# Attention, experts and an MLP on one core: a small add moves from VectorE to ScalarE, and eight low parts and four word steps get other places

## Chip, cores, metric

The kernel runs on one core of one Trainium2 chip. The metric is the device time of one execution in microseconds (us). Engines are named as the profile names them: PE is TensorE's matmul, PEld its weight load, DVE is VectorE, ACT is ScalarE, POOL is GpSimd, SP is SyncE, whose queue issues most DMAs.

## What is computed

Three layers follow one another: attention with 32 global rows and a window of 32, a router with 8 experts of limited capacity, and an MLP. Cut to what matters:

```python
def sm(s):
    e = np.exp(s - np.max(s, axis=-1, keepdims=True))
    return e / (np.sum(e, axis=-1, keepdims=True) + 1e-09)
...
x = attention(q, k, v).transpose(0, 2, 1, 3).reshape(1152, 512)   # 2 batches, 544 + 32 rows
expert = argmax(x @ w_gate, axis=1)                               # 8 experts
# each expert takes its first 288 tokens, in order
h = np.maximum(np.einsum('ecd,edf->ecf', disp, w1), 0.0)          # 512 -> 1024
y = np.einsum('ecf,efd->ecd', h, w2)                              # 1024 -> 512
x = gate * y[expert, position]
h = x @ w_in                                                      # 512 -> 2048
g = np.where(h >= 1, h, np.where(h <= -1, 0.0, (h + 1) ** 2 / 4))
out = g @ w_out                                                   # 2048 -> 512
```

The `1e-09` in the softmax is the number that the change is about; it is added to the sums of the local rows.

## The kernel before

The order of the work is written out by hand; no scheduler moves it, and each engine runs its instructions in the order of the program.

**Attention** (0 to 84 us in the trace) is a loop over 16 steps k (two batches, pairs of row tiles, pairs of heads), with scores of step k+2, exponentials of step k+1, and values of step k-1 beside each other. Two tables, `first[k]` and `plan[k]`, hang further work on a step. One kind of it is routing: `route(k, b, tp)` puts on step k the logits and `recips` (L505 to 508: the softmax sums `SUM` of one row tile, 128 x 16, get 1e-9 added at L507 and are inverted at L508, both on DVE), then `choose` (which expert), and on steps k+1 and k+2 `x_rows` (rows of x, scaled by the inverted sums), `slots` (each token's place), and `scatter` (L566: an indirect DMA on POOL's queue that writes a tile's tokens to `xd` in DRAM, sorted by expert). There are routes at k = 7, 10 and 13, and a last one behind the loop. `x_turn` (L487) transposes attention rows into `px` in PSUM, and `evac_t` (L356) copies transposed tiles out of PSUM.

**Expert weights.** Matmuls run on pairs of a rounded high part and a remainder: a raw weight piece (512 KB, DMA by `weight_load`, L205 on SP) is rounded to `H` (`weight_h`, L218) and `L = raw - H` is taken by `weight_l` (L230, tile 128 x 1024). The pieces of the first expert, `wq[0]` to `wq[7]`, are loaded at steps 2 to 9 and converted at steps 5 to 12, one piece to a step, high part on ACT and low part on POOL. The raw pieces go through four buffers in turn, so a load waits for the low part that used its buffer. Behind the loop `weight_load(2, c)` issues the four pieces of the second expert's first matrix.

**Experts** (92 to 254 us) run one after another. The first expert's tokens `xt0` are read back from `xd` (L714) as soon as the scatters up to (1, 2) have landed; the tokens of the last two tiles go in by a matmul with `place` (L739). `X0` is the pair of high and low part of these tokens, the low part at L744 on DVE. The scatters of the last two tiles, (1, 3) and (1, 4), stand behind it. The second expert's tokens `xt1` (L778, on SP, behind two weight pieces `raw3_0` and `raw3_1`) are turned at L798 (`mx`), which stands in PE's order in the middle of the first expert's second matmul.

**MLP** (254 us to the end) takes its weights from 64-bit floats: `wide_abs` (L248, ACT), four word steps (`wide_words`: L259, L262, L265, L270, DVE, from `raw` over `ca` to `co`; `ca` and `co` have two buffers each), `wide_h` (L280, ACT) and `wide_l` (L285, DVE). The last word steps of pieces 4 and 5 of group 0 hang on the last expert, as the list `ws[2]`, whose last two entries are L270 of these two pieces. Right behind them come the tokens' high parts (L1137, ACT, in two halves) and low parts (L1138, DVE, two instructions, one tile `oldH`), and then the first matmuls `up` (L1156), `half_relu` (L1161), `g_rows`, `g_parts` and `down` (L1196). The low parts of L1138 come into `up` as its last terms.

```python
        if 5 <= k < 13:                      # loop over steps
            c = k - 5
            weight_h(*wq[c], nc.scalar)
            weight_l(*wq[c], nc.gpsimd)
    for c in range(4):                       # behind the loop
        weight_load(2, c)
    recips(1, 3, NB_)
```

Of the kernel before, what the change touches and what calls it, by code (L numbers as in the profile page):

```python
# [8 lines left out]
F32 = mybir.dt.float32  # L9
# [4 lines left out]
AF = mybir.ActivationFunctionType  # L14
# [4 lines left out]
P = 128  # L19
# [9 lines left out]
def tile_attention_moe_ffn(  # L29
# [23 lines left out]
    nc = tc.nc  # L53
# [18 lines left out]
    const = ctx.enter_context(tc.tile_pool(name="const", bufs=1))  # L72
# [14 lines left out]
    def ps_tile(tag, name, hold=False):  # L87

        bank = psum[tag].pop(0)
        (held.setdefault(name, []) if hold else psum[tag]).append(bank)  # L90
        return pspool.tile([P, 512], F32, tag=bank, name=name, bufs=2 if bank == "T" else 1)
# [11 lines left out]
    def ps_v(name, hold=False):  # L103
        return ps_tile("V", name, hold)
# [56 lines left out]
    tri_b = const.tile([P, P], BF16, name="tri_b")  # L161
    ones_b = const.tile([P, P], BF16, name="ones_b")
    half = const.tile([P, 1], F32, name="half")
    racc = const.tile([P, E], BF16, name="racc")
    base_b = const.tile([P, E], BF16, name="base_b")

# [34 lines left out]
    def weight_load(u, c):  # L201
        src, n1 = units[u]
        n = n1 // 4
        raw = raw_tile(f"raw{u}_{c}")
        nc.sync.dma_start(raw.rearrange("p (k f) -> p k f", k=n), src[:, c * n:(c + 1) * n, :])  # L205
        RAW[u, c] = raw
# [15 lines left out]
    def weight_h(u, c, eng):  # L222
        if c == 0:
            unit_tiles(u, units[u][1])
        round_to(eng, HL[u][0][:, c * 1024:(c + 1) * 1024], RAW[u, c])

    def weight_l(u, c, eng):
        H, L = HL[u]
        sl = slice(c * 1024, (c + 1) * 1024)
        eng.tensor_tensor(out=L[:, sl], in0=RAW.pop((u, c)), in1=H[:, sl].bitcast(F32), op=ALU.subtract)  # L230
# [273 lines left out]

    def recips(b, lo, hi):  # L505
        sv = SUM[b][:, lo - 1:hi - 1, :]
        nc.vector.tensor_scalar_add(sv, sv, 1e-9)  # L507
        nc.vector.reciprocal(sv, sv)  # L508

    def choose(b, lo, hi):  # L510
# [90 lines left out]
    def consts():  # L601
        nc.gpsimd.tensor_copy(tri_b, tri_f)
        nc.gpsimd.memset(ones_b, 1.0)
        nc.gpsimd.memset(half, 0.5)
        nc.gpsimd.memset(racc, 0.0)
        nc.gpsimd.tensor_scalar(out=base_b, in0=iota_sb[:, :E], scalar1=float(XS), scalar2=None, op0=ALU.mult)
        for b in range(B):
            nc.gpsimd.memset(LG[b], 0.0)
            nc.gpsimd.memset(M8[b], 0.0)
            nc.gpsimd.memset(I8[b], 255)  # L610
# [33 lines left out]
    wq = [(u, c) for u in range(2) for c in range(4)]  # L644
# [14 lines left out]
    def route(k, b, tp):  # L659

        lo, hi = (0, 3) if tp == 0 else (3, 5)
        i = 2 * tp + 1
        x = [lambda j=j: x_rows(b, j) for j in range(lo, hi)]
        sc = [lambda j=j: scatter(b, j) for j in range(lo, hi)]
        first[k] += [lambda: logits(b, i, 2), lambda: recips(b, i, i + 2)]
        plan[k] += [lambda: logits_t(b, i, 2)]
        if tp == 0:
            first[k].append(lambda: logits(b, 0, 1))
            plan[k].append(lambda: logits_t(b, 0, 1))
        plan[k] += [lambda: choose(b, lo, hi)]  # L670
        first[k + 1] += x[:1]
        plan[k + 1] += [lambda: slots(b, lo, hi)] + x[1:2] + sc[:1]
        plan[k + 2] += x[2:] + sc[1:]

    route(7, 0, 0)
    route(10, 0, 1)
    route(13, 1, 0)
    plan[NS - 1] += [lambda hp=hp: last_logits(hp) for hp in range(NHP - 2)]
    for k in range(NS):
        if 0 < k < NS - 1:  # L680
            exps(k + 1)
        if 0 < k < NS - 2:
            scores(k + 2)
        for f in first[k]:
            f()
        transp(k)
        evac_t(k)
        if k > 0:
            av(k - 1)
        for f in plan.get(k, ()):  # L690
            f()
        if 2 <= k < 10:
            weight_load(*wq[k - 2])
        if 5 <= k < 13:
            c = k - 5
            weight_h(*wq[c], nc.scalar)
            weight_l(*wq[c], nc.gpsimd)
    for c in range(4):
        weight_load(2, c)
    recips(1, 3, NB_)  # L700
    for i in (3, 4):
# [43 lines left out]
    for i in (3, 4):  # L745
        scatter(1, i)

    pc = ps_v("pcnt")
    nc.tensor.matmul(pc[:1, :E], ones_b[:, 0:1], racc, start=True, stop=True)
    cnt = const.tile([1, E], I32, name="cnt")  # L750
# [239 lines left out]
    def job_l(u, c):  # L990
        weight_l(u, c, nc.vector)
        if wn[0] < len(wl) + 6:
# [8 lines left out]
    ws = [wide_words((0, 2 * c), (0, 2 * c + 1)) for c in range(3)]  # L1001
    hl = [[lambda c=c: wide_h(0, c), lambda c=c: wide_l(0, c)] for c in range(4)]
    ab = [lambda c=c: wide_abs(0, c) for c in range(8)]
    WIDE = {
        E - 2: [[], [], [], [], [], [], ab[:2], ws[0][:4]],
        E - 1: [ws[0][4:], ab[2:3], hl[0] + ab[3:4] + ws[1][:2], hl[1] + ws[1][2:4], ws[1][4:6], ws[1][6:],
                ab[4:6] + hl[2] + hl[3], ws[2]],
    }
    own = {1: [own_start], 2: [next_w], 3: [next_w], 4: [lambda: own_ones(0)], 5: [own_gated, next_w],
           6: [lambda: own_matrix(0), next_w]}  # L1010
# [122 lines left out]
    for h in range(2):  # L1133
        px = OWN["x"][h].rearrange("p (k n) -> p k n", k=2)
        xh, xl = (x.rearrange("p (a h) n -> p h a n", h=2)[:, h] for x in XC[0])
        for i in range(2):
            nc.scalar.copy(xh[:, i], px[:, i])  # L1137
        nc.vector.tensor_tensor(out=xl, in0=px, in1=xh.bitcast(F32), op=ALU.subtract)  # L1138

    nfl = fq // P  # L1140
    assert nfl == len(parts)
# [267 lines left out]
```

## Time and profile before

| | us |
|---|---|
| median of 3 runs | 464.36 |
| the three runs | 463.87 to 465.65 |
| the profiled execution's own time | 465.16 |
| its span in the trace | 463.4 |

| stretch of the trace | what runs |
|---|---|
| 0 to 84 us | attention, with routing and the first expert's weights |
| 84 to 92 us | the last tokens' routing, first expert's tokens |
| 92 to 254 us | eight experts |
| 254 to 463 us | MLP |

How to read the rows below. A row of the timeline gives start and length in us, engine, line, operation, tiles out<-in, and how many instructions were put together; in brackets is the idle time before it on its engine and what ended it. A row by stretches gives the stretch, its length, the busy us of each engine (with instructions in brackets), then the granted clock of TensorE as a share of full speed, the busy share of the DMA engines and GB/s. A row of DMA issues gives KB and median us from issue to landing. In a row of DMA landings the three numbers are least, median and most.

### The profile page before, as it was taken

To read this page: it belongs to the slowest core of one execution; us is meant where nothing else is said; L and a number is where in the kernel's file an instruction comes from. 1 tells how busy PE (TensorE), PEld (TensorE's weight loads), DVE (VectorE), ACT (ScalarE), POOL (GpSimd) and SP (SyncE) were. 2 spreads that over 40 slices of the span, in tenths; PEclk is the share of its full clock that TensorE was granted. 3 is DMA by queue.
4 is the path that set the end of the run, shared out by engine and by line. 5 is a ranking of instruction groups with operands and counts; after the bars stand their busy time and mean duration, and the time that the engine had idled before them with its cause. 6 is when DMAs were issued, how large, how long until landed. Compare 5 with 4: busy or idle time off the path is not lost. (4 is left out here: it accounts for less than half of the span.)

```text
span 463.4 us, 8110 instructions
## 1 busy us (share of the span) xinstructions
PE 445.2 (96%) x2875; PEld 375.6 (81%) x2876; DVE 335.9 (72%) x715; ACT 242.6 (52%) x508; POOL 95.5 (21%) x98
## 2 busy tenths in 40 slices
PE   8998989999999999999999899998999999999997
PEld 4876777787577777777777799998999899999996
DVE  3787698584157389946898976687888988879633
ACT  4869666173145478726766575645344344533321
POOL 1105365300000000000001543232133131322321
PEclk9999999999999999999999899999999999999999
DMA  8999554589439189963987340562321410000103
GB/s 271 298 330 340 204 181 138 172 302 374 141 123 317 34 278 343 383 248 117 341 298 243 98 149 0 201 208 93 91 75 63 136 47 1 0 2 0 69 0 127
DMA packets 34595, 79.17 MB, mean 171 GB/s; under 512 B 3761, under 2 KB 8497, under 8 KB 34546
## 3 DMA queue, kind: packets, MB, share of 16 engines
q1 hardware_dynamic: 31698, 70.40, 44.4%
q0 software_dynamic: 1408, 4.46, 3.0%
q10 hardware_dynamic: 1440, 3.67, 2.2%
q8 instruction: 29, 0.48, 0.4%
q14 instruction: 20, 0.16, 0.1%
HBM read 63.77 MB, written 14.75 MB: 169 GB/s over the span
## 5 line engine op out<-in xcount | busy, mean ns | idle before, releaser
L1156 PE MATMUL fh<-oldH,H 128*128 128x256 f32 (+1 forms) x256 | 65.9, 333 | 3.4 <-DVE oldH L1138 1.7
L230 DVE TENSOR_TENSOR L<-raw,H 128x1024 fp32r<-128x1024 f32 x56 | 66.3, 1218 | 0.9 <-ACT H L218 0.6
L1196 PE MATMUL acc<-oldH,H 128*128 128x256 f32 (+2 forms) x240 | 65.0, 332 | 1.4 <-ACT H L280 1.0
L218 ACT CAST H<-raw 128x1024 fp32r<-128x1024 f32 x57 | 58.0, 1049 | 10.3 <-PEq L895 8.4
L1156 PEld LDWEIGHTS fh<-oldH,H 128*128 128x128 f32 x256 | 46.0, 195 | 6.6 <-DVE oldH L1138 2.2
L1170 DVE SCALAR_TENSOR_TENSOR r<-r 128x256 f32<-128x256 f32 (+2 forms) x48 | 31.8, 662 | 22.1 <-ACT r L1161 21.7
L1196 PE MATMUL acc<-oldH,L 128*128 128x256 f32 (+2 forms) x144 | 47.3, 328 | 0.0
L1182 ACT CAST oldH<-g 128x256 fp32r<-128x256 f32 (+2 forms) x36 | 17.9, 496 | 55.8 <-DVE g L1174 55.8
L1196 PEld LDWEIGHTS acc<-oldH,H 128*128 128x128 f32 x240 | 43.3, 189 | 4.2 <-ACT H L280 1.5
L1156 PE MATMUL fh<-oldH,L 128*128 128x448 f32 (+1 forms) x128 | 42.3, 331 | 0.0
L1183 POOL TENSOR_TENSOR oldH<-g,oldH 128x256 fp32r<-128x256 f32 (+2 forms) x24 | 26.5, 1104 | 74.6 <-ACT oldH L1182 59.1
L599 DVE TENSOR_TENSOR hl<-pt,hh 128x512 fp32r<-128x512 f32 (+1 forms) x24 | 15.7, 654 | 35.6 <-ACT hh L598 35.6
L860 PE MATMUL py<-H,hh 128*128 128x512 f32 (+1 forms) x96 | 38.7, 403 | 0.0
L1161 ACT ACTIVATE r<-fh,half 128x256 f32<-128x256 f32 (+2 forms) x48 | 27.1, 564 | 20.6 <-PE fh L1156 17.8
L860 PE MATMUL py<-L,hh 128*128 128x512 f32 (+1 forms) x96 | 37.6, 392 | 0.0
L285 DVE TENSOR_TENSOR L<-co,H 128x512 fp32r<-128x512 f32 x32 | 23.2, 730 | 18.1 <-ACT H L280 17.4
L845 ACT ACTIVATE hs<-ph 128x512 f32<-128x512 f32 (+1 forms) x24 | 14.4, 598 | 41.2 <-PE ph L842 41.2
L1156 PE MATMUL fh<-oldL,H 128*128 128x384 f32 x128 | 35.3, 340 | 0.1
L931 POOL DMA_INDIRECT yg_own<-yd,idx x2 | 2.3, 1156 | 148.5 <-DVE hl L599 148.2
L324 ACT ACTIVATE sm<-sm,ng 128x224 f32<-128x224 f32 x64 | 30.1, 476 | 4.6 <-DVE ng L313 4.6
L270 DVE SCALAR_TENSOR_TENSOR co<-raw,ca 128x512 uint32<-128x512 uint32 x32 | 31.6, 995 | 0.9
L860 PE MATMUL py<-H,hl 128*128 128x512 f32 (+1 forms) x96 | 28.5, 401 | 0.0
(202 smaller groups left out, 1019.4 us busy)
## 6 DMA issues: line engine op xcount, KB each, us to landing
raw<-in_w_dram SPq DMA_DIRECT2D x64, 512.0 KB, 5.9
raw<-in_w_in_dram SPq DMA_DIRECT2D x14, 512.0 KB, 5.0
raw<-in_w_out_dram SPq DMA_DIRECT2D x12, 512.0 KB, 3.7
xd<-zero SPq DMA_DIRECT2D x16, 256.0 KB, 6.0
vt<-in_vx_dram SPq DMA_DIRECT2D x8, 320.0 KB, 5.0
xt<-xd SPq DMA_DIRECT2D x8, 256.0 KB, 6.3
yd<-zero SPq DMA_DIRECT2D x8, 256.0 KB, 3.8
yd<-ys SPq DMA_DIRECT2D x8, 256.0 KB, 5.2
```

What stands on the lines that cost most here:

```text
L218: nc.scalar.copy(dst, src)
L230: eng.tensor_tensor(out=L[:, sl], in0=RAW.pop((u, c)), in1=H[:, sl].bitcast(F32), op=ALU.subtract)
L270: nc.vector.scalar_tensor_tensor(out=o, in0=lo, scalar=29, in1=a, op0=ALU.logical_shift_right, op1=ALU.bitwise_or)
L285: nc.vector.tensor_tensor(out=L[:, sl], in0=CV.pop((g, c)), in1=H[:, sl].bitcast(F32), op=ALU.subtract)
L324: nc.scalar.activation(SM[s][:, c, :], SM[s][:, c, :], AF.Exp, bias=NG[s][:, c:c + 1], scale=-1.0, accum_out=SUM[b][:, i, col:col + 1])
L860: nc.tensor.matmul(py[:rows], h[:, 4 * q + k, :rows], w[:, 4 * q + k, :], start=q == i == 0, stop=q == 1 and i == len(terms) - 1)
L1156: nc.tensor.matmul(ph[:, :n], w[:, k, :], XC[c][i // 2][:, k, :], start=n_ == 0, stop=n_ == len(terms) - 1)
L1161: nc.scalar.activation(RS[f % 2][:, :n], ph[:, :n], AF.Relu, bias=half, scale=0.5)
L1170: nc.vector.scalar_tensor_tensor(out=r[:, :n], in0=r[:, :n], scalar=1.0, in1=r[:, :n], op0=ALU.min, op1=ALU.mult)
L1182: nc.scalar.copy(gh[:, :n], gt[:, :n])
L1183: nc.gpsimd.tensor_tensor(out=gl[:, :n], in0=gt[:, :n], in1=gh[:, :n].bitcast(F32), op=ALU.subtract)
L1196: nc.tensor.matmul(a[:, :n], p[:, ds], q, start=f == 0 and i == 0, stop=f == nfl - 1 and i == 2)
```

## The change

Four edits. (1) The add of 1e-9 in `recips`, four times in the program, becomes an activation on ACT (Identity, with a bias tile `tiny` that POOL fills once at the start); the reciprocal stays on DVE. (2) The high and low parts of the first expert's pieces move from steps 5 to 12 to steps 5, 6, 8, 9, 11, 12, 14 and 15, so that steps 7, 10 and 13, where routes begin, have none. The eighth low part goes to DVE, behind `X0`. (3) `weight_load(2, 3)`, whose buffer this eighth low part frees, follows it. (4) The last word step of pieces 4 and 5 moves behind the low parts L1138.

```diff
+    tiny = const.tile([P, 1], F32, name="tiny")
...
     def recips(b, lo, hi):
         sv = SUM[b][:, lo - 1:hi - 1, :]
-        nc.vector.tensor_scalar_add(sv, sv, 1e-9)
+        nc.scalar.activation(sv, sv, AF.Identity, bias=tiny)
         nc.vector.reciprocal(sv, sv)
...
+        nc.gpsimd.memset(tiny, 1e-9)
...
+    conv_at = [5, 6, 8, 9, 11, 12, 14, 15]
     route(7, 0, 0)
     route(10, 0, 1)
     route(13, 1, 0)
...
-        if 5 <= k < 13:
-            c = k - 5
+
+        if k in conv_at:
+            c = conv_at.index(k)
             weight_h(*wq[c], nc.scalar)
-            weight_l(*wq[c], nc.gpsimd)
-    for c in range(4):
+            if c < 7:
+                weight_l(*wq[c], nc.gpsimd)
+    for c in range(3):
         weight_load(2, c)
...
     for i in (3, 4):
         scatter(1, i)
 
+    weight_l(*wq[7], nc.vector)
+    weight_load(2, 3)
...
-                ab[4:6] + hl[2] + hl[3], ws[2]],
+                ab[4:6] + hl[2] + hl[3], ws[2][:6]],
...
         nc.vector.tensor_tensor(out=xl, in0=px, in1=xh.bitcast(F32), op=ALU.subtract)
+    for f in ws[2][6:]:
+        f()
```

Lines behind the edits stand one or more lines lower in the kernel after (L566 is L567 there, L230 is L231, L1138 is L1145).

**POOL, steps 9 to 16 of attention.** `raw1_0` to `raw1_3` are the pieces `wq[4]` to `wq[7]`; `xr10` is tile 0 of batch 1. Before:

```order
L566 DMA xd_77<-xr02_917,sidx_138 16384x512
L230 TENSOR_TENSOR L1_928<-raw1_0_661,H1_927 128x1024
L230 TENSOR_TENSOR L1_928<-raw1_1_746,H1_927 128x1024
L566 DMA xd_77<-xr03_1023,sidx_138 16384x512
L230 TENSOR_TENSOR L1_928<-raw1_2_863,H1_927 128x1024
L566 DMA xd_77<-xr04_1089,sidx_138 16384x512
L230 TENSOR_TENSOR L1_928<-raw1_3_925,H1_927 128x1024
L566 DMA xd_77<-xr10_1219,sidx_138 16384x512
L566 DMA xd_77<-xr11_1268,sidx_138 16384x512
L566 DMA xd_77<-xr12_1301,sidx_138 16384x512
```

After:

```order
L567 DMA xd_77<-xr02_917,sidx_139 16384x512
L231 TENSOR_TENSOR L0_583<-raw0_3_580,H0_582 128x1024
L567 DMA xd_77<-xr03_1019,sidx_139 16384x512
L231 TENSOR_TENSOR L1_1091<-raw1_0_663,H1_1090 128x1024
L567 DMA xd_77<-xr04_1085,sidx_139 16384x512
L231 TENSOR_TENSOR L1_1091<-raw1_1_748,H1_1090 128x1024
L567 DMA xd_77<-xr10_1217,sidx_139 16384x512
L231 TENSOR_TENSOR L1_1091<-raw1_2_863,H1_1090 128x1024
L567 DMA xd_77<-xr11_1266,sidx_139 16384x512
L567 DMA xd_77<-xr12_1301,sidx_139 16384x512
```

A low part now stands between the scatters of `xr10` and `xr11`, where before the three stood together, and the pair of low parts behind `xr02` is one.

**SP, behind the loop.** `xt0` and `xt1_0` are the first and second expert's tokens, `raw2_*` and `raw3_*` the second expert's weight pieces. Before:

```order
L205 DMA raw2_2_1318<-in_w1_dram 128x1024
L205 DMA raw2_3_1320<-in_w1_dram 128x1024
L714 DMA xt0_1352<-xd_77 128x512
L205 DMA raw3_0_1452<-in_w2_dram 128x2x512
L205 DMA raw3_1_1454<-in_w2_dram 128x2x512
L778 DMA xt1_0_1456<-xd_77 128x512
L205 DMA raw3_2_1458<-in_w2_dram 128x2x512
```

After:

```order
L206 DMA raw2_2_1319<-in_w1_dram 128x1024
L719 DMA xt0_1351<-xd_77 128x512
L206 DMA raw2_3_1431<-in_w1_dram 128x1024
L206 DMA raw3_0_1454<-in_w2_dram 128x2x512
L206 DMA raw3_1_1456<-in_w2_dram 128x2x512
L785 DMA xt1_0_1458<-xd_77 128x512
L206 DMA raw3_2_1460<-in_w2_dram 128x2x512
```

`raw2_3` moved behind `xt0`; it waits for the eighth low part, and `raw3_0`, `raw3_1` and `xt1_0` are queued behind it.

**DVE, end of the last expert and start of the MLP.** `ca0_4` to `ca0_6` and `co0_4`, `co0_5` are word tiles of pieces 4 to 6, `po0` and `po1` the tokens in PSUM, `oldH2` where their parts go. Before:

```order
L265 SCALAR_TENSOR_TENSOR ca0_5_3984<-raw16_5_3628,ca0_5_3984 128x512
L270 SCALAR_TENSOR_TENSOR co0_4_4006<-raw16_4_3601,ca0_4_3982 128x512
L270 SCALAR_TENSOR_TENSOR co0_5_4008<-raw16_5_3628,ca0_5_3984 128x512
...
L1138 TENSOR_TENSOR oldH2_4227<-po0_4016,oldH2_4227 128x2x256
L1138 TENSOR_TENSOR oldH2_4227<-po1_4017,oldH2_4227 128x2x256
L259 TENSOR_SCALAR ca0_6_4306<-ca0_6_4306 128x512
```

After:

```order
L1145 TENSOR_TENSOR oldH2_4225<-po0_4014,oldH2_4225 128x2x256
L1145 TENSOR_TENSOR oldH2_4225<-po1_4015,oldH2_4225 128x2x256
L271 SCALAR_TENSOR_TENSOR co0_4_4243<-raw16_4_3603,ca0_4_3984 128x512
L271 SCALAR_TENSOR_TENSOR co0_5_4245<-raw16_5_3630,ca0_5_3986 128x512
L260 TENSOR_SCALAR ca0_6_4308<-ca0_6_4308 128x512
L263 TENSOR_SCALAR ca0_6_4308<-ca0_6_4308 128x512
```

The two last word steps changed places with the two low parts; `ca0_6`, which takes the buffer of `ca0_4`, still follows both.

## Rows read from the trace of the kernel before

**Rows 1.** Page, part 1: busy time of each engine.

```profile
PE 445.2 (96%) x2875; PEld 375.6 (81%) x2876; DVE 335.9 (72%) x715; ACT 242.6 (52%) x508; POOL 95.5 (21%) x98
```

**Rows 2.** Chain that ended last: start us, us, engine, tile, line.

```profile
258.25 6.30 PE fh L1156 x38
```

**Rows 3.** Timeline of PE, attention: the two longest waits that bear on routing.

```profile
42.87 1.03 PE L308 MATMUL sp<-kr,qr 64*128 64x224 f32 x8 [1.81 <-DVE m L532]
...
62.91 0.66 PE L487 MATMUL px<-ident,xT 128*128 128x128 f32 x4 [1.58 <-DVE xT L356]
```

**Rows 4.** Timeline of PE, start of the MLP.

```profile
257.65 1.22 PE L1156 MATMUL fh<-oldH,H 128*128 128x256 f32 x5 [1.68 <-DVE oldH L1138]
```

**Rows 5.** Stretches: busy us of PE, PEld, DVE, ACT, POOL; clock, DMA, GB/s.

```profile
44.00:48.00 4.00, 4.00 (x38) 3.59 (x36) 2.77 (x10) 1.41 (x4) 0.81 (x1) 0.57 1.05 405
...
64.00:68.00 4.00, 4.00 (x74) 3.43 (x71) 3.68 (x20) 1.58 (x3) 0.05 (x1) 1.00 0.58 185
74.00:78.00 4.00, 3.86 (x45) 3.02 (x42) 3.90 (x18) 2.94 (x11) 1.14 (x1) 1.00 0.75 271
...
258.00:264.00 6.00, 5.91 (x37) 5.75 (x36) 5.46 (x11) 2.08 (x5) 4.36 (x5) 0.72 0.49 134
```

**Rows 6.** Timeline of DVE: three adds, one reciprocal, one comparison of `choose`.

```profile
39.42 1.30 DVE L507 TENSOR_SCALAR ssum<-ssum 128x16 f32<-128x16 f32 x1
...
43.52 1.33 DVE L536 TENSOR_TENSOR oh<-iota_sb,i 128x24 bf16<-128x24 f32 x1
...
59.16 2.54 DVE L507 TENSOR_SCALAR ssum<-ssum 128x16 f32<-128x16 f32 x1
...
61.73 0.25 DVE L508 RECIPROCAL ssum<-ssum 128x16 f32<-128x16 f32 x1
...
73.33 1.85 DVE L507 TENSOR_SCALAR ssum<-ssum 128x16 f32<-128x16 f32 x1
```

**Rows 7.** Timeline of POOL: low parts beside the second add.

```profile
59.27 4.78 POOL L230 TENSOR_TENSOR L<-raw,H 128x1024 fp32r<-128x1024 f32 x2
```

**Rows 8.** Timeline of ACT: copy ahead of the second route's sums.

```profile
58.14 0.36 ACT L455 COPY ls<-lt 128x256 f32<-128x256 f32 x1
```

**Rows 9.** DMA issues, 36.0 to 36.4 us: KB, us to landing.

```profile
kr<-in_kd_dram SPq DMA_DIRECT2D x1, 304.0 KB, 5.9
```

**Rows 10.** Timeline of POOL: scatters of batch 1, tiles 1 and 2.

```profile
81.41 0.99 POOL L566 DMA_INDIRECT xd<-xr,sidx  x1 [0.31 <-DVE pT L339]
...
82.99 0.97 POOL L566 DMA_INDIRECT xd<-xr,sidx  x1 [0.59 <-issue]
```

**Rows 11.** Timeline of SP: the reads of both experts' tokens.

```profile
85.72 0.33 SPq L714 DMA_DIRECT2D xt<-xd  x1
...
94.92 0.34 SPq L778 DMA_DIRECT2D xt<-xd  x1
```

**Rows 12.** Landings: xt, 84 to 98 us; then two weight pieces issued 95.2 to 96.1.

```profile
DMA to landing us min/median/max: 2.9/2.9/2.9
...
DMA to landing us min/median/max: 4.6/5.5/6.4
```

**Rows 13.** Timeline of PE: where each expert's tokens are first read.

```profile
89.84 1.11 PE L739 MATMUL px<-ident,xt 128*128 128x128 f32 x8
...
100.92 0.60 PE L798 MATMUL mx<-ident,xt 128*128 128x128 f32 x4
```

**Rows 14.** Timeline of DVE: low part of the first tokens, and low parts after it.

```profile
92.51 0.69 DVE L744 TENSOR_TENSOR x0l<-px,x0h 128x512 fp32r<-128x512 f32 x1 [2.53 <-ACT x0h L743]
...
93.46 2.36 DVE L230 TENSOR_TENSOR L<-raw,H 128x1024 fp32r<-128x1024 f32 x2 [0.19 <-ACT H L218]
```

**Rows 15.** Timeline of DVE, start of the MLP.

```profile
255.41 1.28 DVE L270 SCALAR_TENSOR_TENSOR co<-raw,ca 128x512 uint32<-128x512 uint32 x2
...
256.91 1.29 DVE L1138 TENSOR_TENSOR oldH<-po,oldH 128x512 fp32r<-128x512 f32 x2 [0.21 <-ACT ca L248]
...
269.72 0.68 DVE L1131 TENSOR_TENSOR oldL<-p,oldL 128x512 fp32r<-128x512 f32 x1
```

## The prediction, made before the kernel after was run

> **What bounds the kernel now.** I read the busy times first [rows 1]: PE works 445.2 of 463.4 us, so a change can only bring back PE's 18 us of waits, or time in which its clock is low. The chain of waits comes next: from 258.25 us it runs over PE, beginning with 6.3 us of the MLP's first matmuls [rows 2]. So I went through PE's waits in its timeline, and then looked at who is late for each. Two lie where the change works in attention: 1.81 us at 42.87 and 1.58 us at 62.91 [rows 3]. One lies at the start of the MLP: 1.68 us before 257.65, for L1138 [rows 4]. The third view is the table by stretches [rows 5], where the reader sees two places with PE busy nearly all the time at a low granted clock (a mean over its two levels, 2.4 GHz as 1.00 and 1.2 GHz as 0.50): 0.57 in 44 to 48 us, behind the 1.81 us wait, and 0.72 in 258 to 264 us, behind the 1.68 us wait. Behind the 1.58 us wait the clock stays at 1.00 in 64 to 68 us.
>
> **The adds of 1e-9.** An add on 128 x 16 numbers lasted 1.30, 2.54 and 1.85 us on DVE in the first three routes [rows 6]. The second began at 59.16 while two low parts on POOL ran from 59.27 to 64.05 [rows 7], and ended at 61.70, when the first of the two (2.39 us) was over. The reciprocal on the same numbers took 0.25 us at 61.73 [rows 6], with POOL's second low part running. So the add is held by POOL's low part, and the reciprocal is not. The Trainium skill, "SBUF — State Buffer", section "Who interferes with whom", says the same: a DVE instruction in a two-port mode, or one with two SBUF inputs, waits for a GpSimd instruction that reads SBUF, for all of its length, and one with at most one SBUF input outside such modes does not. The trace agrees at both instructions.
>
> Second route (k = 10): PE's 1.58 us wait is for a copy L356 that stands on DVE behind the add and the reciprocal [rows 3]. After, the add runs on ACT behind the copy `ls`, which ends at 58.50 [rows 8]; the trace has no such activation, and by the nearest row, that copy of 128 x 256, it takes at most 0.36 us, so the sums are there by 58.9, before DVE comes to the reciprocal at 59.16. DVE reaches L356 some 2.5 us earlier, which is more than PE's wait. Gain: 1.6, all of the wait; the bounds are 0, if another DVE instruction is held in its place (rival D), and 1.6.
>
> Third route (k = 13): the add was held for 1.85 us [rows 6], but PE idles only 0.14 us in 74 to 78 us [rows 5]. The gain lies between 0.14 and 1.6 (1.85 less 0.25 for an undisturbed instruction of that size). I take 0.3, near the row on PE, with as much again for matmul ends that are only modelled.
>
> First route (k = 7): nothing. The add took 1.30 us at 39.42, but PE's 1.81 us wait there ends at 42.87 with the scores, whose `kr`, 304 KB issued at 36.2 us, takes 5.9 us to land [rows 9], at 42.1; the queries come after it on the same queue. This wait, and the low clock behind it, stay, whatever DVE does. The fourth add, behind the loop, has no low part beside it; I cost it at nothing.
>
> **The low parts that move.** POOL has seven low parts of 2.39 us instead of eight, spread over more steps. What is late by them is at the end of attention: the scatters of tiles 1 and 2 of batch 1 began at 81.41 and 82.99 [rows 10], and POOL was free from 81.10 (81.41 less 0.31 idle). Now the low part of piece 6 stands ahead of both, as the order shows. They begin at about 83.5 (81.1 + 2.4) and, one scatter (0.99) and at most the idle 0.59 later, at 84.5 to 85.1: the second is 1.5 to 2.1 us later, and so is its landing. The read of `xt0` goes out at 85.72 [rows 11], behind this landing; it moves to 87.2 to 87.8, and with 2.9 us to land [rows 12] the tokens are there at 90.1 to 90.7. PE first reads them at 89.84 [rows 13], and the matmuls behind stand in order, so nothing hides it. Loss: 0.3 to 0.9, or 0 if POOL runs further ahead once attention is shorter by the second route's 1.6; I take 0.6, the middle of what the rows give.
>
> **Piece 7 and the queue on SP.** Its low part, 1.2 us on DVE (half of 2.36), stands behind L744, which ends at 93.20 [rows 14]. It ends at 94.4. DVE's next work, two low parts, shifts by that; DVE then waits for ACT and PE, so this is hidden. But `raw2_3` on SP waits for it, and behind `raw2_3` stand `raw3_0`, `raw3_1` and `xt1`; before, these pieces were issued already and `xt1` went out at 94.92, landing 2.9 us later at 97.8 [rows 11, 12]. PE reads it at 100.92 [rows 13], so there were 3.1 us to spare. After, three issues of some 0.4 us stand ahead, so `xt1` is issued at about 95.7, behind 1.5 MB. At the 405 GB/s of a full stretch [rows 5] a 512 KB piece takes 1.3 us, so three take 3.9. If `xt1` comes right behind them it lands at 94.4 + 2.2 (2.9 less its own transfer of 0.65) + 3.9 + 0.65 = 101.2; if it shares with the two pieces behind it, all is there at 103.8. A pair of pieces issued just then took 4.6 and 6.4 us [rows 12], which gives 100.3 and 102.1. Against 100.92 that is a loss of 0 to 2.9; I take 1.1 (102.0), by the row of the pair's second, since all pieces are in flight together.
>
> **The MLP's start.** L1138 came behind two L270 (255.41, 1.28 us) and then lasted from 256.91 to 258.20 [rows 15]; PE waited for it until 257.65 [rows 4]. With the exchange L1138 begins at about 255.4, 1.5 us earlier, and PE's wait falls to about 0.2. But the work is only exchanged: the two L270 still come ahead of the words of piece 6, and DVE is busy 5.46 of 6.0 us in 258 to 264 [rows 5]. The third low part of the next tokens at 269.72 [rows 15] then gates PE's next matmuls at about the same time as before, because it comes at the end of an order that hardly got shorter: DVE's idle 0.21 ahead of L1138 [rows 15] is about all that is filled. What PE gains ahead of 264 it gives back in waits for DVE up to 270. Gain: 0.3. Bounds: 1.5 and half of the clock's loss on top if PE keeps its lead (0.28 of 6 us is 1.7; together up to 3.2), and a loss of 0.5 if the later `co` tiles hold up ACT and, through it, the MLP's second matmuls.
>
> **The sum**, on the profiled execution's 465.16 us: -1.6 - 0.3 + 0.6 + 1.1 - 0.3 = -0.5, so 464.7; the median is 0.8 lower than that execution, so 463.9.
>
> **Rivals.**
> A. The MLP's lead reaches the end. For it: PE's wait of 1.68 us is the largest single one that the exchange meets, and the chain lies on PE from there [rows 2]; the low clock comes behind that wait. Against: DVE is full until 270. Gain 3.2 instead of 0.3: 463.9 - 2.9 = 461.0.
> B. The two transfers are hidden: POOL starts earlier and `xt1` lands before 100.9. For it: xt1 has 3.1 us to spare. Then 1.7 of loss falls away: 462.2.
> C. Slower. `xt1` lands last, behind the whole batch of pieces, at 103.8. PE waits 2.9 us in the middle of the first expert, and behind a wait of that length its clock goes down, as it did behind 1.81 us [rows 3, 5]: 0.43 of 4 us is 1.7. Price 2.9 + 1.7 = 4.6 in place of 1.1: 463.9 + 3.5 = 467.4. It decides from a wait between 1.58 us, behind which the clock stayed up, and 1.68 us, behind which it fell: `xt1` at 102.5 or later. Against: 102.0 is the value by the nearest row.
> D. The adds do move but bring nothing: the time held goes to the next DVE instruction with two SBUF inputs, such as the comparison of `choose`, 1.33 us for 128 x 24 numbers [rows 6], or the reciprocal waits for ACT, whose queue has exponentials ahead. One low part still stands near 59 us. Then 1.9 of gain is lost: 465.8. The skill's section named above makes this likely for two-input instructions alone; against it, the copy L356 that PE waits for comes ahead of the comparison.
>
> **How the numbers follow.** The forecast, 463.9 with its own range of 462.7 to 465.1, has 0.46; A 0.15, B 0.15, C 0.12, D 0.12. For 8 in 10 the range takes in B and D whole, and A and C in part: 461.3 to 466.5. 0.5%, about what a measurement of this kernel can tell from no change, is 2.3 us, so faster is below 462.0 and slower above 466.7. A is faster, and a half of B with some of the MLP's gain: 0.22. C and a part of D with late transfers: 0.14. The rest, 0.64, is the same.
>
> **What would show it.** In the profile after: no wait of PE near 62 for L356, and no add on DVE (the steps on the adds); PE's wait for `kr` near 42.9 unchanged; the scatters of tiles 1 and 2 of batch 1 behind a low part, and a wait of about 0.6 us ahead of the `xt` matmuls near 89; `raw2_3` issued behind DVE's low part, and a wait of about 1.1 us ahead of `mx` near 101; a short wait ahead of the first L1156, the clock of the following 6 us above 0.72, and new waits of PE for DVE up to 270. I would be wrong if PE waits for something new in the steps between 63 and 90 us (the low parts now also lie in steps 14 and 15), if `mx` stalls for more than 1.7 us, or if the MLP's lead is still there at 270.

## The result, and the profile after

The changed kernel takes 470.42 us (median of 4, 469.03 to 471.03) against 465.0 (median of 4, 463.87 to 465.97): ratio 1.0114, 95% interval 1.0084 to 1.0143. It is 5.4 us slower, where 463.9 was forecast; the range ended at 466.5. The profiled execution after took 469.03 us with a span of 467.2, so its trace holds 3.8 us of the loss (the span before is 463.4). Executions more than 1.5% above the fastest of their kernel are left out of ratios and intervals, which touches two of e4_low67 below and no other.

The timeline of PE in the kernel after, four places (the line is `start us, us, engine line, operation, tiles [idle before <- what ended it]`):

```profile
49.15 1.12 PE L368 MATMUL g<-kr,qgt 64*32 64x288 f32 x16 [1.76 <-DMA qgt<-in_qg_dram]
...
62.46 0.66 PE L488 MATMUL px<-ident,xT 128*128 128x128 f32 x4
...
90.69 1.16 PE L744 MATMUL px<-ident,xt 128*128 128x128 f32 x8 [1.67 <-DMA xt<-xd]
...
104.24 0.66 PE L805 MATMUL mx<-ident,xt 128*128 128x128 f32 x4 [0.66 <-DMA xt<-xd]
```

The wait of 1.58 us ahead of `px` in [rows 3] is gone (62.46 has no bracket). In its place stands one of 1.67 us for the first expert's tokens, which had none in [rows 13], and one of 0.66 us for the second expert's. The same matmuls, placed against those of before, say how the time runs: at 78.02 of before PE is 0.87 us ahead, at 85.65 it is 1.21 ahead, at 89.84 it is 0.84 behind, at 93.38 it is 2.38 behind, and at 100.92 (the first `mx`) 3.31 behind. Most of the loss arises in those 15 us; the lag goes on to 4.7 at 252.74 and is 3.8 at the end.

What holds the tokens stands on POOL and SP. First the scatter of tile 0 of batch 1 on POOL before, which stands just ahead of [rows 10]:

```profile
80.22 0.88 POOL L566 DMA_INDIRECT xd<-xr,sidx  x1 [5.08 <-DVE xr L501]
```

Timeline of POOL, then of SP, in the kernel after, at the places of [rows 10] and [rows 11]:

```profile
79.36 0.87 POOL L567 DMA_INDIRECT xd<-xr,sidx  x1 [4.67 <-DVE xr L502]
80.25 2.38 POOL L231 TENSOR_TENSOR L<-raw,H 128x1024 fp32r<-128x1024 f32 x1
82.78 1.00 POOL L567 DMA_INDIRECT xd<-xr,sidx  x1 [0.17 <-DVE xr L502]
84.09 0.97 POOL L567 DMA_INDIRECT xd<-xr,sidx  x1 [0.31 <-DVE xT L357]
```

```profile
82.65 0.33 SPq L206 DMA_DIRECT2D raw<-in_w_dram  x1
87.94 0.33 SPq L719 DMA_DIRECT2D xt<-xd  x1
95.53 0.81 SPq L206 DMA_DIRECT2D raw<-in_w_dram  x2
...
97.21 0.34 SPq L785 DMA_DIRECT2D xt<-xd  x1
```

The low part of piece 6 stands between the scatters, as foreseen, and the last scatter ends at 85.06 instead of 83.96: 1.1 us later. But `xt0` is read at 87.94 instead of 85.72: 2.2 us later. From the end of the last scatter's instruction to the read it was 1.76 us before, and is 2.88 now. At 82.65, the moment the low part ends, SP issues `raw2_2`, the weight piece whose buffer it frees.

The stretches behind the two waits, in the kernel after (busy us of PE, PEld, DVE, ACT, POOL, then clock, DMA share, GB/s):

```profile
88.00:92.00 4.00, 2.33 (x20) 2.19 (x20) 0.99 (x2) 0.00 (x0) 0.58 (x1) 1.00 0.29 66
92.00:96.00 4.00, 3.95 (x15) 2.66 (x14) 2.35 (x4) 2.54 (x4) 1.56 (x3) 0.57 0.35 133
...
258.00:264.00 6.00, 5.42 (x36) 4.65 (x35) 5.61 (x12) 2.98 (x8) 1.50 (x2) 1.00 0.21 64
```

The stretch behind 92 before:

```profile
92.00:96.00 4.00, 3.95 (x19) 3.00 (x17) 3.12 (x4) 2.96 (x6) 0.91 (x2) 1.00 0.54 189
```

PE is busy for 2.33 of the 4 us ahead of 92, and then works at a mean clock of 0.57, near the lower of the two levels (1.2 of 2.4 GHz); before, the same stretch ran at 1.00. That costs the step from 0.84 to 2.38 us behind. In 258 to 264, on the other hand, the clock is 1.00 where [rows 5] had 0.72, and PE still has nothing of it in the end. The mean clock is 0.993 in both traces: before has its low stretches in 44 to 48 and 258 to 264 us, after in 52 to 56 and 92 to 96 us.

### The profile page after: what moved, and what is told of

Same layout as the page of the kernel before. It is cut to its first block, busy times and chain, and to the rows that moved or that the text cites. A ratio compares the mean times of both kernels' runs of the same rounds, so it can differ in the third digit from the quotient of the medians.

```text
span 467.2 us, 8106 instructions
## 1 busy us (share of the span) xinstructions
PE 447.0 (96%) x2875; PEld 374.8 (80%) x2876; DVE 330.1 (71%) x712; ACT 243.3 (52%) x512; POOL 92.9 (20%) x98
## 5 line engine op out<-in xcount | busy, mean ns | idle before, releaser
L231 DVE TENSOR_TENSOR L<-raw,H 128x1024 fp32r<-128x1024 f32 x57 | 67.5, 1218 | 0.7 <-ACT H L219 0.4
L1165 PE MATMUL fh<-oldH,H 128*128 128x256 f32 (+1 forms) x256 | 64.7, 328 | 2.6 <-DVE g L1183 1.6
L1165 PEld LDWEIGHTS fh<-oldH,H 128*128 128x128 f32 x256 | 44.8, 189 | 6.1 <-DVE g L1183 1.8
L600 DVE TENSOR_TENSOR hl<-pt,hh 128x512 fp32r<-128x512 f32 (+1 forms) x24 | 15.7, 654 | 36.4 <-ACT hh L599 36.4
L849 PE MATMUL ph<-H,x0h 128*128 128x512 f32 x64 | 27.2, 425 | 1.8 <-PEq L902 1.3
```

Source lines behind the costliest of these rows:

```text
L849: nc.tensor.matmul(HP[q][:rows], x[:, k, :rows], w[:, k, fs], start=i == 0, stop=i == len(terms) - 1)
L1165: nc.tensor.matmul(ph[:, :n], w[:, k, :], XC[c][i // 2][:, k, :], start=n_ == 0, stop=n_ == len(terms) - 1)
```

## The experiments

All were compared with the kernel before on the same chip; its median in the three groups was 464.9, 464.7 and 465.4 us, and 465.1 for the last single run. Differences between experiments of two groups are therefore best taken from the ratios.

| run | edit | median us | ratio to before | 95% interval |
|---|---|---|---|---|
| e1_add | before + edit 1 | 463.36 | 0.9977 | 0.9952 to 1.0002 |
| e2_spread | edits 2 and 3 alone | 469.44 | 1.0122 | 1.0096 to 1.0148 |
| e3_words | before + edit 4 | 464.43 | 1.0005 | 0.9982 to 1.0029 |
| e4_low67 | after, low parts 6, 7 on POOL behind the scatters | 467.93 | 1.0044 | 1.0014 to 1.0073 |
| e9_one_low | before, one low part between the scatters | 470.16 | 1.0120 | 1.0090 to 1.0151 |
| e12_low_noload | e9, freed load behind `xt0` | 466.72 | 1.0029 | 1.0007 to 1.0051 |
| e6_warm | after, dummy matmuls in the wait | 468.78 | 1.0077 | 1.0051 to 1.0103 |
| e5_xt1 | after, `raw2_3` behind `xt1` | 466.75 | 1.0050 | 1.0024 to 1.0077 |
| e10_xt1_warm | both | 466.15 | 1.0005 | 0.9980 to 1.0031 |
| e7_dve67 | after, low parts 6, 7 on DVE | 466.01 | 1.0021 | 0.9996 to 1.0045 |
| e8_add_words | before + edits 1 and 4 | 464.21 | 0.9979 | 0.9951 to 1.0007 |
| e11_loads | e8, loads ahead of zero fills | 461.16 | 0.9900 | 0.9865 to 0.9936 |

### Which edit it is

**e1_add**, the kernel before with the add on ACT:

```diff
-        nc.vector.tensor_scalar_add(sv, sv, 1e-9)
+        nc.scalar.activation(sv, sv, AF.Identity, bias=tiny)
```

> The kernel before with the add on ACT alone (first edit). Theory P (the loss comes from the late read of the first expert's tokens, behind the low part of piece 6 on POOL, and from the clock that falls behind that wait): none of this is in this kernel, so only the gain of the adds is left, about 1.5 us at the second route and 0.3 to 0.7 at the third: 463.0 to 464.2 against 465.0 of before. Rival R (the add on ACT itself moves attention into a new wait, such as the one for the global queries near 49 us, with a low clock behind it): 466 to 467.

463.36 us: theory P's value, and R falls. The interval reaches 1.0002, so that it is faster than before is likely, not proven. The comparison of `choose` at 62.43 lasts 2.32 us in this trace, beside POOL's low part of 62.36 to 64.72: the time held does go to the next instruction with two SBUF inputs, as rival D had it. But the copy L357 stands ahead of it, at 60.17, and PE's wait at `px` is gone.

**e2_spread**, the kernel after with the first and fourth edits taken back:

```diff
-        nc.scalar.activation(sv, sv, AF.Identity, bias=tiny)
+        nc.vector.tensor_scalar_add(sv, sv, 1e-9)
...
-                ab[4:6] + hl[2] + hl[3], ws[2][:6]],
+                ab[4:6] + hl[2] + hl[3], ws[2]],
```

> The kernel after with the add back on DVE and the words back ahead of the low parts, so that only the second and third edits (the spread of the low parts, and the load of raw2_3) are left. P: nearly all of the loss is here: 468.5 to 471, with a wait of 1 to 1.7 us for xt near 90 us and a clock near 0.6 in the 4 us behind it. R: the loss belongs to the add, so 464.5 to 466.

469.44 us: the whole loss is in the moved low parts and the moved load (pieces 2 to 7 change their step, six of the title's eight). Its ratio, 1.0122, stands beside 1.0114 of after, which has the add's gain as well: whether that gain reaches the end behind the spread can't be told within these intervals. Its trace has a wait of 1.57 us for `xt` at 92.88.

**e3_words**, the kernel before with the exchange at the start of the MLP:

```diff
-                ab[4:6] + hl[2] + hl[3], ws[2]],
+                ab[4:6] + hl[2] + hl[3], ws[2][:6]],
...
         nc.vector.tensor_tensor(out=xl, in0=px, in1=xh.bitcast(F32), op=ALU.subtract)
+    for f in ws[2][6:]:
+        f()
```

> The kernel before with the fourth edit alone (two low parts ahead of the last word step of pieces 4 and 5). If the lead that PE gets at the start of the MLP (some 2.6 us) is given back to words and gathered rows by 270 us, as the trace of after reads: 464.5 to 465.5. If the lead is real and only hidden by other losses: 462 to 463.

464.43 us, ratio 1.0005: nothing. Its trace shows where the lead goes. Against before, PE's lead grows by 2.35 us, to 3.10, between 252.74 and 262.01, and by 268.13 it is down by 1.6 again, 1.0 of it in three waits (timeline of PE, e3_words):

```profile
260.10 0.39 PE L1158 MATMUL fh<-oldH,H 128*128 128x256 f32 x1 [0.43 <-DVE g L1176]
...
263.81 1.27 PE L1122 MATMUL p<-ident,oldL 128*128 128x128 f32 x8 [0.44 <-ACT oldL L1113]
...
266.67 0.66 PE L1122 MATMUL p<-ident,oldL 128*128 128x128 f32 x4 [0.15 <-DVE oldL L1110]
```

They are for DVE's and ACT's work, which is only 0.6 to 1.3 us earlier than before (DVE's `g` at 259.62 for 260.22, its L1110 at 265.87 for 267.19), less than PE's lead.

### What in the spread does it

**e9_one_low**, the kernel before with one low part two steps later on POOL:

```diff
-            weight_l(*wq[c], nc.gpsimd)
+            if c < 7:
+                weight_l(*wq[c], nc.gpsimd)
+        if k == 14:
+            weight_l(*wq[7], nc.gpsimd)
```

> The kernel before with one thing changed: the low part of piece 7 is issued on POOL two steps later, at step 14, so that it stands between the scatters of batch 1, tiles 0 and 1, as piece 6 does in after. Theory P (a low part there costs the wait for xt and the clock behind it): the read of xt0 goes out 2 us later, PE waits about 1 us near 90 us and the clock falls for some 4 us behind it in most executions: 466.5 to 468.5 against 464.9 of before. Rival Q (the loss needs the longer queue of weight pieces on SP): 464.5 to 465.5.

470.16 us, above P's range: this one instruction, 2.4 us long, costs as much as the whole change, together with the load that waits for it. In its trace PE is 1.15 us behind before already at 85.65, from a low clock in 48 to 56 us that the edit doesn't touch, and 6.1 behind at the first `mx`. The trace (PE, then the stretches behind):

```profile
92.78 1.18 PE L742 MATMUL px<-ident,xt 128*128 128x128 f32 x8 [1.63 <-DMA xt<-xd]
```

```profile
92.00:96.00 4.00, 3.22 (x18) 2.76 (x18) 0.00 (x0) 0.40 (x2) 1.94 (x2) 0.72 0.94 336
96.00:100.00 4.00, 3.95 (x11) 2.85 (x10) 3.11 (x4) 2.14 (x3) 0.98 (x2) 0.50 0.38 113
```

The wait is that of after, and the low clock lasts about twice as long. In the third edit's absence the second expert's tokens don't wait, so Q isn't needed for the loss.

**e12_low_noload**, the same with the load that this low part frees behind the read of `xt0`:

```diff
-    for c in range(4):
+    for c in range(3):
         weight_load(2, c)
...
     nc.sync.dma_start(xt0, xd[0:P, :])
+    weight_load(2, 3)
```

> The kernel before with the low part of piece 7 at step 14 on POOL, as in the run with one low part, but with the load raw2_3, which that low part sets free, behind the read of xt0 on SP instead of ahead of it. In all traces with a low part between the scatters xt0 goes out 2.7 to 2.9 us after the last scatter's instruction, in the others 1.7 to 1.8. Theory P1 (the freed weight piece moves while the scatters write, and makes them land 1.0 to 1.1 us later): the gap falls back to 1.8 us, PE's wait near 90 us to under 0.7 us, the clock stays up in most executions, and the time is 465.5 to 467. Theory P2 (the order on POOL alone does it, the gap belongs to the scatters being close together): the gap stays at 2.7, 469 to 471.

466.72 us, P1. Timelines of POOL, SP and PE in e12_low_noload:

```profile
83.76 0.97 POOL L566 DMA_INDIRECT xd<-xr,sidx  x1 [0.30 <-DVE xr L501]
```

```profile
86.49 0.33 SPq L717 DMA_DIRECT2D xt<-xd  x1
```

```profile
89.09 1.16 PE L743 MATMUL px<-ident,xt 128*128 128x128 f32 x8 [0.41 <-DMA xt<-xd]
```

The read goes out 1.76 us after the last scatter's end (84.73), exactly as before. So the 2.2 us by which `xt0` was late in after are two things of equal size: 1.1 us of POOL's order, and 1.1 us that the freed weight piece adds to the scatters' landing. Together they make a wait of 1.6 us; without the piece PE waits 0.41 us, the clock stays up in 88 to 96 us, and of the 5.4 us by which e9 was over its before 1.6 are left. The 1.6 us by which it is still slower than before would be covered by that wait and one of 1.19 us at 96.80, which ACT ends; this was not taken apart further.

**e4_low67**, the kernel after with the low parts of pieces 6 and 7 on POOL behind the scatters:

```diff
-            if c < 7:
+            if c < 6:
                 weight_l(*wq[c], nc.gpsimd)
+    for c in (6, 7):
+        weight_l(*wq[c], nc.gpsimd)
...
     nc.sync.dma_start(xt0, xd[0:P, :])
+    for c in (2, 3):
+        weight_load(2, c)
...
-    weight_l(*wq[7], nc.vector)
-    weight_load(2, 3)
```

> The kernel after with the low parts of pieces 6 and 7 both on POOL behind the scatters of batch 1, tiles 1 and 2, and the loads of raw2_2 and raw2_3 behind the read of xt0; nothing else is changed. P: the scatters go out as early as before, the wait of 1.7 us for xt and the low clock behind it are gone, 3 us or more less than after: 466 to 467.5. Rival Q (the queue on SP and the second expert's late tokens cost most): only about 0.5 to 1 us less than after: 469.5 to 470.

467.93 us in the median of all twelve executions, a little above P's range, and 466.98 us in that of the ten that the ratio takes, inside it. `xt0` is read early, at 84.51, 1.77 us after the last scatter, and the wait for it is gone; but a new one takes its place (POOL, DVE and PE of e4_low67):

```profile
82.76 4.66 POOL L231 TENSOR_TENSOR L<-raw,H 128x1024 fp32r<-128x1024 f32 x2
```

```profile
85.62 1.84 DVE L537 TENSOR_TENSOR oh<-iota_sb,i 128x16 bf16<-128x16 f32 x1
```

```profile
87.52 0.17 PE L552 MATMUL pc<-oh,tri_b 128*128 128x8 bf16 x1 [1.51 <-DVE oh L537]
```

The comparison of the last `choose`, 0.17 us long in after, starts while POOL's low parts run and ends with them. It has two inputs in SBUF, as rival D had it, and it stands on PE's path here. The Trainium skill, "SBUF — State Buffer", section "Who interferes with whom", says that such an instruction contends with a GpSimd instruction that reads SBUF, and calls the shared port pair an exclusive lock; the trace agrees, 1.84 against 0.17 us. Behind the 1.51 us PE's clock is 0.56 in 88 to 92 us. Single executions among the ten went from 463.43 (mean clock 1.00) to 470.25 (0.981): that fits a wait that doesn't bring the clock down in all of them, though only one has a trace.

### The clock, and the second wait

**e6_warm**, the kernel after with dummy matmuls where PE waits for `xt0`:

```diff
             x, at_ = parts[n]
+            if n == 2:
+                keep_warm(7)
             for k in k0:
```

> The kernel after with seven more dummy matmuls (128 x 512, bf16, about 0.21 us each at full clock) ahead of the xt matmuls, in the time in which PE waits for xt0. P: the wait is for a DMA and stays in length, but PE is busy through it, so the clock does not fall behind it and the 1.4 us of low clock in 92 to 96 us come back: 468 to 469. If the clock falls for another reason than the wait: as after, 469.5 to 470.5.

468.78 us, in P's range. The stretches of e6_warm:

```profile
92.00:96.00 4.00, 4.00 (x25) 3.15 (x24) 2.04 (x4) 2.54 (x4) 1.91 (x2) 1.00 0.35 133
104.00:108.00 4.00, 3.53 (x11) 2.95 (x12) 1.81 (x3) 2.43 (x4) 0.00 (x0) 0.57 1.04 376
```

Behind the filled wait the clock stays at 1.00. But PE, earlier by that, now waits longer for the second expert's tokens, whose time is set by SP:

```profile
104.47 1.06 PE L807 MATMUL mx<-ident,xt 128*128 128x128 f32 x4 [1.93 <-DMA xt<-xd]
```

Behind these 1.93 us the clock is 0.57 in 104 to 108 us. In this trace the gain is given back within 16 us.

**e5_xt1**, the kernel after with `raw2_3` read behind `xt1`:

```diff
     weight_l(*wq[7], nc.vector)
-    weight_load(2, 3)
+    held = raw_tile("raw2_3")
+    RAW[2, 3] = held
...
     x_load(1, 0, 1)
+    nc.sync.dma_start(held.rearrange("p (k f) -> p k f", k=units[2][1] // 4), units[2][0][:, 3 * (units[2][1] // 4):, :])
```

> The kernel after, with the DMA of raw2_3 behind the read of the second expert's tokens on SP instead of ahead of raw3_0 and raw3_1. P: xt1 goes out and lands 1 to 2 us earlier, the wait of 0.66 us ahead of the first mx goes, but the wait for xt0 and the clock stay: 0.8 us less than after, 468.5 to 470. Q: the queue is most of the loss: 466 to 467.5.

466.75 us, in Q's range: 3.7 less than after (0.6%, or 3.0, by the ratios) and far beyond P's 0.8. `raw3_0` and `raw3_1` go out at 87.88 again, `xt1` is issued at 95.20 and lands 2.5 us later, and no wait is left ahead of `mx`. P had taken the 0.66 us of after's single trace as the price of the second wait; e6_warm shows it at 1.93 us with a low clock behind it. Three of the four executions of after had a mean clock of 0.985 against 0.993 for the one with the trace, and took 1.1 to 2.0 us more. That the second wait brings the clock down in these fits, but no trace of them shows it.

The trace of e5_xt1 is of its third slowest execution, 468.83 us (the wait, then the stretches behind it):

```profile
90.26 2.08 PE L744 MATMUL px<-ident,xt 128*128 128x128 f32 x8 [1.58 <-DMA xt<-xd]
```

```profile
88.00:92.00 4.00, 2.42 (x16) 2.28 (x14) 0.66 (x2) 0.00 (x0) 0.97 (x1) 0.63 0.82 273
92.00:96.00 4.00, 3.95 (x16) 2.86 (x16) 1.34 (x2) 2.02 (x4) 1.60 (x3) 0.50 0.48 187
96.00:100.00 4.00, 4.00 (x12) 3.17 (x11) 2.81 (x4) 0.52 (x1) 0.36 (x1) 0.59 0.77 229
```

With the first wait and the low clock behind it alone, PE goes from 1.3 us ahead of before at 88.92 to 4.6 behind at 100.92, more than in the trace of after. Nine of the twelve executions had a mean clock of 0.989 or more, against 0.985 here, so the median stands for executions with less low clock, and how much of after's loss is the second wait stays open. The parts don't close either: e9_one_low, with the first wait alone, loses 1.2%, and e5_xt1, with the first wait and edit 1's gain of 0.2%, only 0.5%.

**e10_xt1_warm**, both edits:

> The kernel after with both of the two earlier edits: raw2_3 read behind the second expert's tokens, and seven dummy matmuls in the wait for xt0. If the loss of after is the wait for xt0, the clock behind it and the second wait at mx, and the dummy matmuls' gain was given back at mx: with both, only the wait for xt0 itself is left, 464.5 to 466. If the two edits bring the same thing twice: no better than the better one alone, 466.5 to 467.

466.15 us, just above the first range, ratio 1.0005: no difference from before can be measured. In its trace the wait for `xt0` is filled but for 0.19 us, and none is left at `mx`. By the ratios the two edits are worth 0.6% and 0.4% alone and 1.1% together, so they add up within the intervals; by the medians (3.7, 1.6 and 4.3 us) they bring a little less together than the sum. With both, the cost of edits 2 and 3 is about what edit 1 gains.

**e7_dve67**, the kernel after with the low parts of pieces 6 and 7 on DVE:

```diff
-            if c < 7:
+            if c < 6:
                 weight_l(*wq[c], nc.gpsimd)
-    for c in range(3):
+    for c in range(2):
         weight_load(2, c)
...
+    for c in (6, 7):
+        weight_l(*wq[c], nc.vector)
+        weight_load(2, c - 4)
     px0 = ps_t("px0")
...
-    weight_l(*wq[7], nc.vector)
-    weight_load(2, 3)
```

> The kernel after with the low parts of pieces 6 and 7 on DVE behind the late tokens' low parts (L734), where DVE idles for 4.7 us in after, each followed by the load that it frees; nothing on POOL between the scatters. P: xt0 is read early, no wait for it, no low clock, and no collision of POOL with a comparison of DVE as in the kernel with both low parts on POOL: 463 to 465. Q: the pieces raw2_2 and raw2_3 now go out after 90 us, ahead of xt1, so the wait ahead of mx stays or grows: 465.5 to 467.5.

466.01 us, in Q's range, but not by Q's mechanism. Neither the wait for `xt0` nor one at `mx` is in its trace; what its trace does have is 3.15 us ahead of the global queries' matmuls at 49.11, with a clock of 0.50 in 48 to 56 us, which the experiment doesn't touch. So it tells that the tokens' waits are gone, and not what the rest is.

### What is worth keeping

**e8_add_words**, the kernel before with edits 1 and 4, the diffs of e1_add and e3_words together.

> The kernel before with the add on ACT and the words behind the low parts, the first and fourth edits, without the moved low parts. If the two add up: 462.5 to 463.5 (1.5 us and 0.2 to 0.5 less than before). If the words cost something beside the add: 464 to 465.

464.21 us, which as a number lies in the second range; but before stood at 465.38 in this group, and by the ratio, 0.9979 (up to 1.0007), it is the add's gain again (e1_add: 0.9977), and nothing from the words either way.

**e11_loads**, the same with the last two units' loads ahead of that step's zero fills on SP's queue:

```diff
-        plan[u - 1] += [lambda u=u: load_unit(u), lambda u=u: load_values(u)]
+        plan[u - 1][:0] = [lambda u=u: load_unit(u), lambda u=u: load_values(u)]
```

> The same with the loads of the last two attention units (keys, queries, values, global queries) ahead of that step's zero fills on SP. In most traces PE waits 1.3 to 3.2 us for the global queries near 49 us, and its clock is low in 50 to 56 us. If that wait sets this stage: the queries land 1.5 to 2.5 us earlier, wait and low clock go, and runs scatter less: 460 to 462. If the transfer is bound by the DMA engines' full load in 40 to 48 us rather than by its place: as without, 462.5 to 463.5.

461.16 us, ratio 0.9900 (0.9865 to 0.9936): faster than both kernels. The global queries, in e1_add and then in e11_loads (PE, then two stretches of each):

```profile
48.61 1.12 PE L368 MATMUL g<-kr,qgt 64*32 64x288 f32 x16 [1.60 <-DMA qgt<-in_qg_dram]
```

```profile
48.00:52.00 4.00, 3.39 (x34) 2.34 (x36) 1.99 (x9) 2.08 (x9) 0.00 (x0) 0.87 0.80 297
52.00:56.00 4.00, 4.00 (x33) 3.02 (x32) 2.36 (x10) 1.46 (x6) 3.60 (x3) 0.70 0.07 17
```

```profile
47.24 1.12 PE L368 MATMUL g<-kr,qgt 64*32 64x288 f32 x16 [0.62 <-DMA qgt<-in_qg_dram]
```

```profile
48.00:52.00 4.00, 4.00 (x42) 2.92 (x36) 3.33 (x16) 2.05 (x9) 1.13 (x2) 1.00 0.83 305
52.00:56.00 4.00, 4.00 (x44) 2.87 (x44) 3.79 (x13) 4.00 (x15) 3.38 (x2) 1.00 0.15 35
```

The wait falls by 1 us and the clock behind it stays at 1.00. The kernel that differs by the loads alone, e8_add_words, has no such wait in its trace, but one for the local queries ahead of it, with a low clock behind:

```profile
42.33 1.85 PE L309 MATMUL sp<-kr,qr 64*128 64x224 f32 x8 [1.27 <-DMA qr<-in_qd_dram]
```

```profile
44.00:48.00 4.00, 4.00 (x50) 3.47 (x48) 3.19 (x11) 1.40 (x4) 0.79 (x1) 0.78 1.05 387
```

In e11_loads PE doesn't wait there, and against this trace it gains 1.6 us up to 48.85, which stay to the end. The edit moves four loads, so which of them matters isn't shown. All six executions had a mean clock of 0.999 or 1.000, where e8_add_words went from 0.989 to 1.000.

## Why the prediction was wrong

**The sign was wrong, by the terms of the two experts' tokens.** The forecast put 0.6 us on the first expert's tokens. In the trace after, PE goes from 1.0 us ahead to 0.84 behind there, and loses 1.5 more behind it: some 3.4 us in place of 0.6. Two steps of that term failed, the landing and the clock; a third, the sum, held.

*The landing.* "The second is 1.5 to 2.1 us later, and so is its landing": the scatter's end was later by only 1.1 us, but its landing by 2.2. A low part that moves takes with it the load that waits for its buffer, and I moved that load for piece 7 alone. For piece 6 it went out at 82.65, in the middle of the scatters. e12_low_noload against e9_one_low shows the 1.1 us: 1.76 us from scatter to read without the piece, 2.77 with it (86.24 + 0.97 to 89.98).

*The sum.* The gains ahead, 1.6 + 0.3, were added to a loss worked out on before's clock. That was sound here: PE was 0.87 us ahead at 78.02, and POOL's scatter of tile 0 began 0.86 us earlier as well (79.36 for 80.22). From the start of that scatter to the end of the last one it took 3.74 us before and 5.70 after, 1.96 more, within the forecast's 1.5 to 2.1. So the wait of 1.67 us in place of 0.6 is the landing's 1.1.

*The clock.* Rival C priced a low clock behind a wait, at 4.6 us in place of 1.1, but for the second expert's tokens alone. Its mechanism came true one transfer earlier, behind a wait of 1.67 us, close to the 1.68 that [rows 4] and [rows 5] show. e6_warm shows it in its trace: the same wait with PE busy, and the clock stays up. At `xt0` I called the wait 0.6 us and didn't ask what a wait of 1.6 would do.

**The second expert's tokens: the size was right in the trace by luck, and the term too small.** Forecast 1.1; the lag grows by 0.8 (2.49 to 3.31) at `mx`. But `xt1` was there at 104.2, not at 102.0: it was issued at 97.21 instead of 95.7 and landed 7.0 us later, and PE's own lag of 2.5 us hid the rest. The forecast took this term as separate from the first. `raw2_3` waits for DVE's low part behind `X0`, which ended at 95.48 and not at 94.4, as `X0` was late with `xt0`, and `xt1` is queued behind it. And e5_xt1 is 3.7 us below after (3.0 by the ratios): the term seems to hold a second, possible fall of the clock, which rival C priced and the sum left out.

**The adds: right.** Second route, forecast 1.6: the add on ACT ran from 59.59 to 59.91, the reciprocal on DVE at 59.94, beside POOL's low part of 59.66 to 62.04, and PE's wait was gone (DVE, then ACT, of after):

```profile
59.94 0.25 DVE L509 RECIPROCAL ssum<-ssum 128x16 f32<-128x16 f32 x1 [0.32 <-issue]
```

```profile
59.59 0.32 ACT L508 ACTIVATE ssum<-ssum,tiny 128x16 f32<-128x16 f32 x1
```

Against before, PE goes from 1.2 behind (at 60.30) to 0.44 ahead there. With the low parts spread but the add left on DVE (e2_spread) the add still took 2.53 us at 60.60, and PE's wait at `px` was 0.75: one low part in place of two. Third route, forecast 0.3: 0.43 (0.44 to 0.87 ahead). The forecast's two gains make 1.9; e1_add brought 1.5. Rival D's first half, that time goes to another two-input instruction, didn't happen on this path in after, and did in e1_add, where PE then waits only 0.16 us, at 66.65, and in e4_low67, where it cost the wait of 1.51 us. The reciprocal did wait for ACT at the first route (1.12 us at 40.96), without a cost that the traces show.

**The first route: "nothing" was too simple.** PE's wait for the keys there is not a fixed 1.81 us. The kernel of e3_words has the same work up to 254 us as before, and its trace is 2.27 us ahead at 47.79 and 0.89 at 49.51. So this stage varies between executions by as much as all my terms: in one the clock falls behind the keys (0.57 in 44 to 48 us before), in another behind the global queries (0.66 in 52 to 56 us after). What of after's 2.06 us lead at 47.79 and its loss by 53.44, where it is 1.1 behind, belongs to the change can't be told from one trace each. e11_loads shows that the place of the last units' loads on SP's queue sets this stage.

**The MLP: right.** Two word steps changed places, not the title's four. Forecast 0.3; e3_words shows nothing within 0.3%. The wait ahead of the first L1156 fell from 1.68 to 0.49, the clock stayed up, and PE's lag went from 4.7 down to 2.1 us and back to 4.1 at 270, 1.0 of it in three waits, two of them for ACT and DVE, as the step said.

## What to carry to other kernels

When an instruction moves, list what waits for the buffer that it frees: that transfer moves too, and may meet another one that matters. Work out a gain only up to the next place whose time is set by another engine or a DMA, and ask whether that time moves along: POOL's scatters moved with PE here, while in e6_warm the second expert's tokens didn't, and the gain became a longer wait. And price a wait of PE by its length and by the clock behind it: here 0.41 us left the clock up, and some 1.6 us cost only itself in one place and twice itself or more in another.

## What the runs showed of the hardware that I had not expected

- A 512 KB weight piece in flight beside two indirect scatters, each of a tile of 128 x 512 numbers, put off the read behind them by 1.0 to 1.2 us: 2.74 to 2.95 us after the last scatter's instruction in the traces with it (after, e2, e5, e6, e9, e10), 1.75 to 1.77 in those without (before, e1, e3, e4, e7, e8, e11, e12).
- The clock's fall is not the same in each execution of one kernel, and its length isn't either. Behind 1.67 us it was 0.57 for some 4 us in after, behind 1.63 us 0.72 and then 0.50 over 8 us in e9_one_low, and behind 1.58 us 0.63, 0.50 and 0.59 over 12 us in e5_xt1. Behind 1.58 us at 62.91 before it stayed at 1.00, and behind 1.51 us in e4_low67 it was 0.56 and 0.50. So the border between 1.58 and 1.68 us that rival C took from two rows doesn't exist as such.
